# Softmax on 16 rows a head, bands placed by one-hot matmuls, and the first tokens loaded as fp32 by SyncE: a lightweight convolution with a ReGLU layer behind it

## The chip, the cores and the metric

The kernel runs on one core of one Trainium2 chip. The time is in device microseconds, from launch to end of one execution, and smaller is better. The time before is 772.24 us, the median of three runs (771.73 to 774.05).

A core has five engines that run beside each other and wait for one another by semaphores: PE (TensorE, the matmuls), DVE (VectorE), ACT (ScalarE), POOL (GpSimd) and SP (SyncE, which here only issues DMAs). POOL, SP and ACT each have a DMA queue. A DMA that SP or ACT issues copies without a change of type; one that POOL issues can turn fp32 into fp16 on its way.

## The reference

Each head has seven taps. They go through a softmax and are the weights of a causal convolution along the tokens: one output is the weighted sum of its own token and the six before it. The result goes through a layer with a gate.

```python
# x: (8, 4096, 192), weight: (8, 7); 24 channels to a head
w = np.exp(weight - max over taps); w = w / (sum over taps + 1e-9)
out[b, s, h, g] = sum over k of w[h, k] * x_pad[b, s + k, h, g]      # x_pad has 6 rows of zeros in front
# out as (32768, 192); w_gate, w_val: (192, 1536); w_out: (1536, 192)
y = (np.maximum(out @ w_gate, 0) * (out @ w_val)) @ w_out
```

## The kernel before

**Tiling.** The batch is cut into two halves of four sequences, called streams. A unit is 1024 tokens of both streams; there are 16 units (`NUNIT`), done one after the other. In a unit, `xc` holds the convolution's result in fp16 with channels on partitions: 64 channels of the one stream on partitions 0 to 63 and of the other on 64 to 127, three chunks of 64 channels (`NCH`). So each weight tile `Wg` and `Wv` has to be there twice, on partitions 0 to 63 from HBM and copied to 64 to 127 (`both_halves`, L165).

**One unit on PE.** `gate_val` (L465) runs over two windows of 512 tokens and in each over 12 pieces f of 128 hidden columns. For each f, 6 matmuls with `Wg` and 6 with `Wv` fill two PSUM tiles; ACT makes `gr`, the ReLU of the first (L487), DVE multiplies it by the second into `hT` (L488). Then `project_columns` (L491) multiplies `hT` with `Wo` in three parts, and DVE turns each part out (`turn_out`, L512). The last unit is projected in another form (L534). All PSUM tiles come from one pool of four, each of two banks, and are given out in turn: a tile is free again when the engine that reads it is done.

**Convolution, two ways.** The first two units are convolved on PE: a band matrix for each head holds the taps on seven diagonals, and a matmul with a block of 118 or 128 tokens (112 new ones) gives the sums. For the first unit this is `conv_dense` (L256), once for each window: `conv_dense(0)` ahead of everything, `conv_dense(1)` in `gate_val` ahead of f = 7. For the second unit it is `conv(2)` and `conv(3)` (L294), after which ACT moves the sums (L317) and SP issues transposing DMAs into `xc` (L336). All later units are done in lanes, away from PE: POOL loads `x_e` (L350), copies it into `x_p` (L387), SP issues eight transposing DMAs into `x_r` (L389; one more for the tokens ahead of the unit, from `turned`, L382), ACT and DVE multiply `x_r` by `tap` (L435, L415, L446), POOL adds products (L424). `tap` holds the softmax by channel; twenty small DMAs on SP fill it from `late` (L210), a copy of the softmax that POOL makes.

**The start.** POOL loads x for the first window into `out_s` as fp16 (L94, L101). `wr`, the taps repeated over 32 rows a head, comes on two queues (L112). `softmax` (L180) makes `we`; `prod` and `blk` (L223, L231) spread it over diagonals, with `eye` from POOL; sixteen copies of 32 or fewer rows, ten on DVE and six on ACT (L242, L244), put `blk` into `band`. Meanwhile PE runs sixteen matmuls on zeros (L128). The weights come in five steps of columns (`CUTS`), all issued on POOL; DVE copies the halves of the first two steps, POOL of the others.

**What sets the order.** The schedule is manual: each engine does its instructions in the order in which the program lists them, and a waiting instruction holds up everything behind it on its engine, DMA issues too.

Of the kernel before, what the change touches and what calls it, by code (L numbers as in the profile page):

```python
# [8 lines left out]
FP = mybir.dt.float32  # L9
F16 = mybir.dt.float16  # L10
ACTF = mybir.ActivationFunctionType
# [4 lines left out]
def kernel(  # L16
# [27 lines left out]
    TAPS = [(6, 5, 4), (3, 2), (1, 0)]  # L44
    GSUB = 5


# [25 lines left out]
    def staged(i, j):  # L73
        return stages[i][:, XH * j : XH * (j + 1)]

    def load_x(g):


        bp, toks = GROUPS[g]
        xt = staged(g // 3, g % 3).rearrange("p (j s d) -> p j s d", s=2, d=D)  # L80
        if toks[0] == 0:
            nc.vector.memset(xt[0:32, 0, :, :], 0.0)
        for st in range(2):
            b = bp + NB * st
            jj = int(toks[0] == 0)
            last = toks[-1] == S - SUB or toks[-1] - toks[-2] != SUB
            n_full = len(toks) - jj - int(last)
            lo = toks[jj] - PAD
# [5 lines left out]
            nc.gpsimd.dma_start(out=xt[:, jj : jj + n_full, st, :], in_=src)  # L94
# [5 lines left out]
        for st in range(2 * int(toks[0] == 0)):  # L100
            nc.gpsimd.dma_start(  # L101
                out=xt[PAD:128, 0, st, :], in_=x[bp + NB * st, 0 : 128 - PAD, :]
            )
        return xt

    xts = {}
    xts[0] = load_x(0)

    HQ = H // 4
    wr = const.tile([128, HQ, KW], FP)  # L110
    for half, eng in ((0, nc.sync), (1, nc.scalar)):
        eng.dma_start(  # L112
            out=wr[64 * half : 64 * half + 64],
            in_=bass.AP(
                tensor=weight.tensor,
                offset=weight.offset + 2 * half * HQ * KW,
                ap=[[HQ * KW, 2], [0, 32], [1, HQ * KW]],
            ),
        )
    BW = 32 + PAD  # L120
    ones = const.tile([128, BW + PAD], FP)
    nc.vector.memset(ones[:], 1.0)

    zeros = const.tile([128, 512], F16)
    nc.vector.memset(zeros[:], 0.0)
    ps = psum.tile([128, 2, 512], FP, name="ps")
    for n in range(16):
        nc.tensor.matmul(  # L128
            out=ps[:, n % 2, :], lhsT=zeros[:, 0:128], rhs=zeros[:], start=True, stop=True
        )  # L130

    bands = [const.tile([128, 2 * HQ, SUB], F16, name=f"band{half}") for half in range(2)]
    for half in range(2):
        nc.vector.memset(bands[half][:], 0.0)

    eye = const.tile([128, BW + PAD], FP)
    for q in range(4):
        nc.gpsimd.affine_select(  # L140
            out=eye[32 * q : 32 * q + 32],
            in_=ones[32 * q : 32 * q + 32],
            pattern=[[-1, BW + PAD]],
            compare_op=ALU.is_equal,
            fill=0.0,
            base=PAD,
            channel_multiplier=1,
        )
# [16 lines left out]
    def both_halves(copy, s, dst):  # L165
        cols = slice(CUTS[s], CUTS[s + 1])
        copy(out=dst[64:128, :, cols], in_=dst[0:64, :, cols])  # L167
# [12 lines left out]
    def softmax(e, raw, n):  # L180
        mx = const.tile([128, n, 1], FP, name=f"mx{n}")
        nc.vector.tensor_reduce(out=mx[:], in_=raw[:], axis=mybir.AxisListType.X, op=ALU.max)
        nc.vector.tensor_tensor(
            out=e[:], in0=raw[:], in1=mx[:].to_broadcast([128, n, KW]), op=ALU.subtract
        )
        nc.scalar.activation(e[:], e[:], ACTF.Exp)
        sm = const.tile([128, n, 1], FP, name=f"sm{n}")
        nc.vector.tensor_reduce(out=sm[:], in_=e[:], axis=mybir.AxisListType.X, op=ALU.add)
        nc.vector.tensor_scalar(out=sm[:], in0=sm[:], scalar1=1e-9, scalar2=None, op0=ALU.add)  # L189
        nc.vector.reciprocal(sm[:], sm[:])  # L190
        nc.vector.tensor_tensor(
            out=e[:], in0=e[:], in1=sm[:].to_broadcast([128, n, KW]), op=ALU.mult
        )

    we = const.tile([128, HQ, KW], FP)
    softmax(we, wr, HQ)

    tap = const.tile([128, NCH, KW], FP)

    def load_taps():  # L200
        late = const.tile([128, HQ, KW], FP)
        nc.gpsimd.tensor_copy(out=late[:], in_=we[:])
        for c in range(NCH):
            r0 = 0
            while r0 < 64:
                h = (64 * c + r0) // G
                r1 = min(64, G * (h + 1) - 64 * c)
                for half in range(2):
                    p0 = 32 * (h // HQ)
                    nc.sync.dma_start(  # L210
                        out=tap[64 * half + r0 : 64 * half + r1, c, :],
                        in_=late[p0 : p0 + r1 - r0, h % HQ, :],
                    )
                r0 = r1

    load_taps()
    xts[2] = load_x(2)
    pool_halves(4)

    prod = const.tile([128, HQ, BW, KW], FP)  # L220
    e0 = eye[:, 0:1]
    w0 = we[:, 0:1, 0:1]
    nc.vector.tensor_tensor(  # L223
        out=prod[:],
        in0=bass.AP(tensor=e0.tensor, offset=e0.offset, ap=[e0.ap[0], [0, HQ], [1, BW], [1, KW]]),
        in1=bass.AP(tensor=w0.tensor, offset=w0.offset, ap=[w0.ap[0], [KW, HQ], [0, BW], [1, KW]]),
        op=ALU.mult,
    )
    blk = const.tile([128, HQ, BW, 1], F16)
    with nc.allow_low_precision("one of the terms is not zero"):  # L230
        nc.vector.tensor_reduce(out=blk[:], in_=prod[:], axis=mybir.AxisListType.X, op=ALU.add)  # L231

    for q in range(4):
        for j in range(4):
            s0 = 32 * j - PAD
            lo, hi = max(0, -s0), min(BW, SUB - s0)
            rows = min(32, SUB + PAD - 32 * j)
            src = blk[32 * q : 32 * q + rows, :, lo:hi, 0]
            h0 = q % 2 * HQ
            dst = bands[q // 2][32 * j : 32 * j + rows, h0 : h0 + HQ, s0 + lo : s0 + hi]  # L240
            if j < 2 or (j == 2 and q % 2 == 0):
                nc.vector.tensor_copy(out=dst, in_=src)  # L242
            else:
                nc.scalar.copy(out=dst, in_=src)  # L244

    def band(h):
        return bands[h // (2 * HQ)][0 : SUB + PAD, h % (2 * HQ), :]

# [6 lines left out]

    def conv_dense(g):  # L256


        xt = xts.pop(g)
        if g == 0:  # L260
            xc[0] = xcpool.tile([128, NCH, UNIT], F16, name="xc")
        t0 = GROUPS[g][1][0]
        rows = SUB + PAD
        if g == 0:
            both_halves(nc.vector.tensor_copy, 0, Wg)
            both_halves(nc.vector.tensor_copy, 0, Wv)
        for c in range(NCH):
            ps = psum.tile([128, 2, 512], FP, name="ps")
            for jj in range(GSUB):
                col = SUB * jj  # L270
                n = min(SUB, WIN - col)
                for second in range(2):
                    for st in range(2):
                        for k2 in range(2):
# [6 lines left out]
                                lhsT=xt[0:rows, jj, st, 32 * k : 32 * k + m],  # L281
                                rhs=band(h)[:, 0:n],
                                start=True,
# [3 lines left out]
                            )  # L287
            copy = nc.vector.tensor_copy if c == 1 else nc.scalar.copy
            copy(out=xc[0][:, c, t0 : t0 + WIN], in_=ps[:, 0, :])  # L289
        if g == 0:  # L290
            both_halves(nc.vector.tensor_copy, 1, Wg)
            both_halves(nc.vector.tensor_copy, 1, Wv)

# [259 lines left out]

    conv_dense(0)
    lane_load(2)
# [76 lines left out]
```

## Time and profile before

| what | value |
|---|---|
| median of three runs | 772.24 us (771.73 to 774.05) |
| the profiled run | 772.0 us, span 770.3 us |
| PE busy | 762.6 us, 99% of the span |
| DVE, ACT, POOL busy | 674.6, 596.8, 425.6 us |
| granted PE clock | 1.00 |
| gate and value matmuls of one unit | 31.19 us |
| projection of one unit | 15.65 us |
| first matmul that isn't on zeros | 9.22 us after the span's start |
| first gate matmul | 11.20 us |
| gate and value of the first unit end | 46.39 us |

The span is the profiled execution from first to last instruction; the run's own time has some 1.7 us around it. The page also has the busy share of every engine in 40 slices: PE is at nine tenths or more in all but the first and the last, in which it has 7 and 8. A row of a timeline reads: start, length, engine, line, operation, output and input with their shapes, and in brackets how long the engine stood idle before and what released it. In the chain of waits a row is start, length, and what the end of the program was waiting for then. In a row on one line of the code, the three numbers are the shortest, median and longest duration in ns.

### The profile page before, as it was taken

The page shows a single profiled execution, that of the slowest core. Times are in us where ns is not written, and L with a number is a line of the kernel's source. Part 1 is how long each engine was busy: PE and PEld are TensorE (multiplying, and loading weights), DVE is VectorE, ACT ScalarE, POOL GpSimd, SP SyncE. Part 2 cuts the span into 40 slices and gives each one's busy share as a digit, 9 for nine tenths or more (in the row PEclk, how much of TensorE's full clock was granted, in tenths as well). Part 3 has the DMA queues.
Part 4 walks back from the last instruction along what each step waited for, and adds up shares of the span by engine and source line. Part 5 has one row for each costly group of instructions (what it writes and reads, how often), then busy time and mean ns, then how long its engine had stood idle before and what let it go on. Part 6 is the DMA issues. An engine that isn't in the chain of part 4 may idle for free.

```text
span 770.3 us, 21536 instructions
## 1 busy us (share of the span) xinstructions
PE 762.6 (99%) x9392; PEld 381.7 (50%) x9392; DVE 674.6 (88%) x641; ACT 596.8 (77%) x621; POOL 425.6 (55%) x194
## 2 busy tenths in 40 slices
PE   7999999999999999999999999999999999999998
PEld 3654444444444444444444444444444444444448
DVE  7888989989899898999989899898998989996691
ACT  4798787978879787787877879788796877874471
POOL 9606839286490955919368292863919558091000
PEclk9999999999999999999999999999999999999999
DMA  9955819085290933909147090742909232030302
GB/s 113 124 69 102 127 25 143 2 115 51 52 116 2 133 34 77 90 3 146 21 93 73 21 146 2 115 52 44 122 3 126 41 73 52 3 83 3 83 2 83
DMA packets 123106, 53.20 MB, mean 69 GB/s; under 512 B 88692, under 2 KB 123012, under 8 KB 123012
## 3 DMA queue, kind: packets, MB, share of 16 engines
q1 hardware_dynamic: 84690, 36.99, 29.6%
q0 software_dynamic: 38112, 14.75, 18.7%
q8 instruction: 73, 1.20, 0.7%
q14 instruction: 21, 0.17, 0.1%
q10 hardware_dynamic: 210, 0.10, 0.0%
HBM read 29.50 MB, written 25.17 MB: 71 GB/s over the span
## 4 chain that ended last, share of the span: by engine, by line
PE 97%; DVE 1%; DMA 1%; ACT 0%; issue 0%; DVEq 0%
PE ps L478 65%; PE ps L498 30%; PE ps L534 2%; DMA wr<-in_weight_dram 1%; PE ps L304 0%; DVE band L242 0%; DVE Wg L167 0%; DVE Wv L167 0%; DVE hT L488 0%; ACT gr L487 0%; DVE prod L223 0%; DVE blk L231 0%; DVE xc L289 0%; ACT out_s L545 0%; DVE sm L189 0%
## 5 line engine op out<-in xcount | busy, mean ns | idle before, releaser
L487 ACT ACTIVATE gr<-ps 128x1024 f16<-128x1024 f32 x384 | 392.8, 1023 | 148.4 <-PE ps L478 148.4
L488 DVE TENSOR_TENSOR hT<-gr,ps 128x1024 f16<-128x1024 f16 x384 | 468.8, 1221 | 37.5 <-ACT gr L487 8.9
L424 POOL TENSOR_TENSOR prod<-prod,prod 128x1792 f32<-128x1792 f32 x70 | 278.4, 3977 | 258.2 <-DVE prod L456 212.9
L478 PE MATMUL ps<-xc,Wg 64*128 64x512 f16 x2304 | 314.2, 376 | 0.6 <-DVE hT L488 0.2
L478 PE MATMUL ps<-xc,Wv 64*128 64x512 f16 x2304 | 314.1, 376 | 0.6 <-DVE Wv L167 0.3
L498 PE MATMUL ps<-hT,Wo 128*32 128x512 f16 x4320 | 236.0, 379 | 0.0
L478 PEld LDWEIGHTS <-Wv 64*128 64x128 f16 x2304 | 131.8, 94 | 118.5 <-issue 1.3
L478 PEld LDWEIGHTS <-Wg 64*128 64x128 f16 x2304 | 114.4, 94 | 137.1 <-issue 7.0
L498 PEld LDWEIGHTS <-Wo 128*32 128x32 f16 x4320 | 114.1, 97 | 120.3 <-issue 6.3
L415 ACT ACTIVATE prod<-x_r,tap 128x1024 f32<-128x1024 f16 (+1 forms) x182 | 172.8, 1040 | 0.0
L446 DVE SCALAR_TENSOR_TENSOR acc<-x_r,tap,acc 128x1024 f32<-128x1024 f16 (+1 forms) x140 | 114.0, 873 | 2.8 <-ACT acc L435 2.8
L512 DVE STREAM_TRANSPOSE out_s<-ps 128x1024 f32<-128x1024 f32 x45 | 56.2, 1248 | 33.1 <-PE ps L498 33.1
L424 POOL TENSOR_TENSOR xc<-prod,prod 128x1792 f16<-128x1792 f32 x14 | 55.7, 3982 | 1.1
L387 POOL COPY x_p<-x_e 128x1536 f16<-128x1536 f16 x28 | 40.3, 1466 | 2.0 <-DMA x_e<-in_x_dram 2.0
L350 POOL DMA_DIRECT2D x_e<-in_x_dram x28 | 25.0, 899 | 3.8 <-POOL x_p L387 3.6
L446 DVE SCALAR_TENSOR_TENSOR xc<-x_r,tap,acc 128x1024 f16<-128x1024 f16 (+1 forms) x28 | 23.5, 882 | 0.0
L435 ACT ACTIVATE acc<-x_r,tap 128x1024 f32<-128x1024 f16 (+1 forms) x28 | 21.5, 820 | 0.8 <-DMA x_r<-x_p 0.8
L534 PE MATMUL ps<-Wo,hT 128*128 128x192 f16 x192 | 16.0, 246 | 0.0
L534 PEld LDWEIGHTS <-hT 128*128 128x128 f16 x192 | 15.8, 98 | 0.4 <-issue 0.4
L545 ACT COPY out_s<-ps 128x768 f32<-128x768 f32 (+2 forms) x5 | 3.2, 638 | 12.7 <-PE ps L534 12.7
L545 DVE COPY out_s<-ps 128x192 f32<-128x192 f32 x1 | 0.4, 357 | 13.3 <-PE ps L534 13.3
L456 DVE TENSOR_SCALAR prod<-x_r,tap 128x768 f32<-128x768 f16 x14 | 8.7, 618 | 0.0
(45 smaller groups left out, 66.7 us busy)
## 6 DMA issues: line engine op xcount, KB each, us to landing
out_dram<-out_s SPq DMA_DIRECT2D x63, 384.0 KB
x_e<-in_x_dram POOLq DMA_DIRECT2D x28, 384.0 KB, 10.5
x_r<-x_p SPq DMA_TRANSPOSE x112
out_s<-in_x_dram POOLq DMA_DIRECT2D x4, 240.0 KB, 6.2
out_s<-in_x_dram POOLq DMA_DIRECT2D x4, 192.0 KB, 5.0
Wo<-in_moe_w_out_dram POOLq DMA_DIRECT2D x1, 576.0 KB, 8.8
Wg<-in_moe_w_gate_dram POOLq DMA_DIRECT2D x3, 144.0 KB, 4.4
Wv<-in_moe_w_val_dram POOLq DMA_DIRECT2D x3, 144.0 KB, 4.8
```

The source lines that it names most:

```text
L350: nc.gpsimd.dma_start(out=xe[:, :, st, :, :].rearrange("p j c r -> p j (c r)"), in_=bass.AP(tensor=x.tensor, offset=x.offset + row * D, ap ...
L387: nc.gpsimd.tensor_copy(out=xp[:, :, :, st, :], in_=xe[:, :, st, :, :])
L415: nc.scalar.activation(out=prods[u, k][:, at - LDVE : at - LDVE + n], in_=shifted(u, c, k, t, n), func=ACTF.Copy, scale=tap[:, c, k : k + 1],)
L424: nc.gpsimd.tensor_tensor(out=p0[:] if k < KW - 1 else flat(u)[:, LDVE:FLAT], in0=p0[:], in1=prods.pop((u, k))[:], op=ALU.add,)
L435: nc.scalar.activation(out=accs[u][:, at : at + n], in_=shifted(u, c, 0, t, n), func=ACTF.Copy, scale=tap[:, c, 0:1],)
L446: nc.vector.scalar_tensor_tensor(out=(flat(u) if k == KW - 1 else acc)[:, at : at + n], in0=shifted(u, c, k, t, n), scalar=tap[:, c, k : k ...
L478: nc.tensor.matmul(out=pss[i][:, st, :], lhsT=W[64 * st : 64 * st + 64, c, 128 * f : 128 * (f + 1)], rhs=xcb[64 * st : 64 * st + 64, c, WI ...
L487: nc.scalar.activation(out=gr[:], in_=pss[0][:], func=ACTF.Relu)
L488: nc.vector.tensor_tensor(out=h[:, f], in0=gr[:], in1=pss[1][:], op=ALU.mult)
L498: nc.tensor.matmul(out=ps[32 * s : 32 * s + 32, b, :], lhsT=Wo[:, f, 64 * p + 32 * b : 64 * p + 32 * b + 32], rhs=hs[s // 2][:, f, s % 2, ...
L512: nc.vector.transpose(out=o[:, :, 64 * p : 64 * p + 64].rearrange("p t (b c) -> p b t c", b=2), in_=ps[:].rearrange("p b (t c) -> p b t c" ...
L534: nc.tensor.matmul(out=ps[:, i // 2, D * (i % 2) : D * (i % 2) + D], lhsT=h[:, f, st, 128 * q : 128 * (q + 1)], rhs=Wo[:, f, :], start=(f ...
```

## The change

It works on the start and on what the first unit does beside it.

- The taps `w` are repeated over 16 rows a head (128 rows for 8 heads) by one DMA on ACT's queue. Maximum, `Exp` and sums run on 7 columns; the sum's reciprocal is folded into `blocks`.
- A one-hot matrix `Z` shifts `blocks` on PE: after two matmuls of zeros that open the banks, eight matmuls for each half of the heads add up the bands in two PSUM tiles; DVE copies one half to `bands`, ACT the other. The sixteen small copies are gone.
- The first window's x is loaded as fp32 by SP in five DMAs and cast on ACT (three) and DVE (two). POOL's queue begins with the weights, in other cuts.
- Six matmuls on zeros (`WARM`) instead of sixteen.
- DVE copies the halves of the first weight step only, POOL those of the next four; those of the last 256 columns are copied by two DMAs on SP, ahead of the taps. They wait for the last weight load.
- `tap` is filled from `wn` (ACT) by 32 DMAs of 16 or 8 rows.
- `conv_dense(1)` runs one chunk each ahead of f = 9, 10 and 11; its x is loaded later, one stream at a time; `load_x(2)` stands behind it.

```diff
+    WARM = 6
+    STEPS0 = [1, 0, 2, 3, 4]
+    CONV1 = [9, 10, 11]
...
-    xts[0] = load_x(0)
...
-    for half, eng in ((0, nc.sync), (1, nc.scalar)):
-        eng.dma_start(
-            out=wr[64 * half : 64 * half + 64],
...
+    def load_raw(jj):
+        lo = SUB * jj - PAD
+        p0 = max(0, -lo)
+        nc.sync.dma_start(
+            out=raw[jj][p0 : ROWS[jj], :].rearrange("p (s d) -> p s d", s=2),
...
+    def cast(copy, jj):
+        copy(
+            out=xts[0][0 : ROWS[jj], jj, :, :].rearrange("p s d -> p (s d)"),
+            in_=raw[jj][0 : ROWS[jj], :],
+        )
...
+    nc.scalar.dma_start(
+        out=w[:],
+        in_=bass.AP(tensor=weight.tensor, offset=weight.offset, ap=[[KW, H], [0, HR], [1, KW]]),
+    )
+    for jj in STEPS0:
+        load_raw(jj)
...
-    for n in range(16):
+    for _ in range(WARM):
         nc.tensor.matmul(
-            out=ps[:, n % 2, :], lhsT=zeros[:, 0:128], rhs=zeros[:], start=True, stop=True
+            out=held[:, 0, :], lhsT=zeros[:, 0:128], rhs=zeros[:], start=True, stop=True
...
-    CUTS = [0, 128, 384, 768, 1152, DFF]
+    CUTS = [0, 128, 256, 512, 896, DFF]
+    HALVES = [0, 128, 256, 512, 896, 1280, DFF]
...
-    for s in range(4):
+    for s in range(5):
         load_w(s)
-    xts[1] = load_x(1)
+    pool_halves(1)
+    xts[1] = load_x(1, [0])
     pool_halves(2)
-    load_w(4)
     pool_halves(3)
...
+    load_x(1, [1])
+    pool_halves(4)
...
+    nc.scalar.activation(out=e[:, 0:KW], in_=w[:], func=ACTF.Exp, bias=mx[:])
+    cast(nc.scalar.copy, 1)
+    cast(nc.scalar.copy, 0)
...
+    nc.vector.scalar_tensor_tensor(
+        out=blocks[:],
+        in0=blk[:].to_broadcast([128, H, BW]),
+        scalar=sm[:],
+        in1=mask[:].to_broadcast([128, H, BW]),
+        op0=ALU.mult,
+        op1=ALU.mult,
+    )
+    wn = const.tile([128, KW], FP)
+    nc.scalar.activation(out=wn[:], in_=e[:, 0:KW], func=ACTF.Copy, scale=sm[:])
+    cast(nc.scalar.copy, 2)
...
+    for half, copy in enumerate((nc.vector.tensor_copy, nc.scalar.copy)):
+        for j in range(128 // HR):
+            s0 = HR * j - PAD
+            lo, hi = max(0, -s0), min(BW, SUB - s0)
+            nc.tensor.matmul(
...
+                lhsT=Z[:, 112 - HR * j : 240 - HR * j],
+                rhs=blocks[:, H // 2 * half : H // 2 * (half + 1), lo:hi],
+                start=False,
...
+        copy(
+            out=bands[half][:].rearrange("p h t -> p (h t)"), in_=raised[half][:, 0, 0 : SUB * H // 2]
+        )
+    cast(nc.vector.tensor_copy, 3)
+    cast(nc.vector.tensor_copy, 4)
...
     def load_taps():
-        late = const.tile([128, HQ, KW], FP)
-        nc.gpsimd.tensor_copy(out=late[:], in_=we[:])
+        both_halves(nc.sync.dma_start, 5, Wg)
+        both_halves(nc.sync.dma_start, 5, Wv)
...
-                for half in range(2):
-                    p0 = 32 * (h // HQ)
-                    nc.sync.dma_start(
-                        out=tap[64 * half + r0 : 64 * half + r1, c, :],
-                        in_=late[p0 : p0 + r1 - r0, h % HQ, :],
-                    )
+                for st in range(2):
+                    for a in range(r0, r1, HR):
+                        n = min(HR, r1 - a)
+                        nc.sync.dma_start(
+                            out=tap[64 * st + a : 64 * st + a + n, c, :],
+                            in_=wn[HR * h : HR * h + n, :],
+                        )
                 r0 = r1
...
-            if u == 0 and w == 0 and f == 7:
-                conv_dense(1)
+            if u == 0 and w == 0 and f in CONV1:
+                conv_dense(1, [CONV1.index(f)])
...
-    conv_dense(0)
+    xc[0] = xcpool.tile([128, NCH, UNIT], F16, name="xc")
+    both_halves(nc.vector.tensor_copy, 0, Wg)
+    both_halves(nc.vector.tensor_copy, 0, Wv)
+    conv_dense(0, range(NCH))
+    xts[2] = load_x(2)
```

More of the change, by code (lines that the diff above doesn't have):

```diff
@@ L74, in staged, with load_x @@
         return stages[i][:, XH * j : XH * (j + 1)]
-    def load_x(g):
+    def load_x(g, streams=range(2)):
         bp, toks = GROUPS[g]
         xt = staged(g // 3, g % 3).rearrange("p (j s d) -> p j s d", s=2, d=D)
-        if toks[0] == 0:
-            nc.vector.memset(xt[0:32, 0, :, :], 0.0)
-        for st in range(2):
+        for st in streams:
             b = bp + NB * st
-            jj = int(toks[0] == 0)
             last = toks[-1] == S - SUB or toks[-1] - toks[-2] != SUB
-            n_full = len(toks) - jj - int(last)
-            lo = toks[jj] - PAD
+            n_full = len(toks) - int(last)
+            lo = toks[0] - PAD
             src = bass.AP(
@@ L93, in load_x @@
             )
-            nc.gpsimd.dma_start(out=xt[:, jj : jj + n_full, st, :], in_=src)
+            nc.gpsimd.dma_start(out=xt[:, 0:n_full, st, :], in_=src)
             if last:
@@ L99, in load_x @@
                 )
-        for st in range(2 * int(toks[0] == 0)):
-            nc.gpsimd.dma_start(
-                out=xt[PAD:128, 0, st, :], in_=x[bp + NB * st, 0 : 128 - PAD, :]
-            )
-        return xt
-    xts = {}
-    xts[0] = load_x(0)
-    HQ = H // 4
-    wr = const.tile([128, HQ, KW], FP)
-    for half, eng in ((0, nc.sync), (1, nc.scalar)):
-        eng.dma_start(
-            out=wr[64 * half : 64 * half + 64],
+        return xt
+    xts = {0: staged(0, 0).rearrange("p (j s d) -> p j s d", s=2, d=D)}
@@ L114 @@
+    ROWS = [SUB + PAD, 128, 128, 128, 80]
+    raw = [
+        apool.tile([128, FLAT - LDVE], FP, name=f"prod{jj + 1}")[:, 0 : 2 * D] for jj in range(GSUB)
+    ]
+    def load_raw(jj):
[3 more added lines that the diff above has]
+            out=raw[jj][p0 : ROWS[jj], :].rearrange("p (s d) -> p s d", s=2),
             in_=bass.AP(
-                tensor=weight.tensor,
-                offset=weight.offset + 2 * half * HQ * KW,
-                ap=[[HQ * KW, 2], [0, 32], [1, HQ * KW]],
-            ),
-        )
@@ L120 @@
-    BW = 32 + PAD
-    ones = const.tile([128, BW + PAD], FP)
-    nc.vector.memset(ones[:], 1.0)
+                tensor=x.tensor,
+                offset=x.offset + (lo + p0) * D,
+                ap=[[D, ROWS[jj] - p0], [NB * S * D, 2], [1, D]],
+            ),
+        )
+    def cast(copy, jj):
[3 more added lines that the diff above has]
+        )
+    HR = 128 // H
+    BW = HR + PAD
+    w = const.tile([128, KW], FP)
@@ L124 @@
+    nc.scalar.dma_start(
[4 more added lines that the diff above has]
+        load_raw(jj)
     zeros = const.tile([128, 512], F16)
     nc.vector.memset(zeros[:], 0.0)
-    ps = psum.tile([128, 2, 512], FP, name="ps")
-    for n in range(16):
+    e = const.tile([128, KW + 1], FP)
+    nc.vector.memset(e[:, KW:], 1e-9)
+    Z = const.tile([128, 256], F16)
+    nc.vector.memset(Z[:], 0.0)
+    nc.vector.memset(raw[0][0:PAD, :], 0.0)
@@ new lines @@
+    early = const.tile([128, 1], FP)
+    nc.scalar.activation(out=early[:], in_=e[:, KW:], func=ACTF.Exp)
+    ones = const.tile([128, 128], FP)
+    nc.gpsimd.memset(ones[:], 1.0)
+    eye = const.tile([128, 128], FP)
+    nc.gpsimd.affine_select(
+        out=eye[:],
+        in_=ones[:],
+        pattern=[[-1, 128]],
+        compare_op=ALU.is_equal,
+        fill=0.0,
+        base=0,
+        channel_multiplier=1,
+    )
+    mask = const.tile([128, H, 1], FP)
+    with nc.allow_low_precision("one of the terms is not zero"):
+        nc.vector.tensor_reduce(
+            out=Z[:, 112 : 112 + HR],
+            in_=eye[:].rearrange("p (g i) -> p i g", i=HR),
+            axis=mybir.AxisListType.X,
+            op=ALU.add,
+        )
@@ L128 @@
+    nc.vector.tensor_reduce(
+        out=mask[:, :, 0],
+        in_=eye[:].rearrange("p (g i) -> p g i", i=HR),
+        axis=mybir.AxisListType.X,
+        op=ALU.add,
+    )
+    held = psum.tile([128, 2, 512], FP, name="ps")
+    for _ in range(WARM):
         nc.tensor.matmul(
-            out=ps[:, n % 2, :], lhsT=zeros[:, 0:128], rhs=zeros[:], start=True, stop=True
+            out=held[:, 0, :], lhsT=zeros[:, 0:128], rhs=zeros[:], start=True, stop=True
         )
-    bands = [const.tile([128, 2 * HQ, SUB], F16, name=f"band{half}") for half in range(2)]
+    raised = [psum.tile([128, 2, 512], FP, name="ps") for _ in range(2)]
@@ L133 @@
     for half in range(2):
[L134 to L147, printed above, removed]
+        nc.tensor.matmul(
+            out=raised[half][:, 0, 0 : SUB * H // 2],
+            lhsT=zeros[:, 0:128],
+            rhs=zeros[:, 0 : SUB * H // 2],
+            start=True,
+            stop=False,
+            skip_group_check=True,
@@ L165, in both_halves @@
     def both_halves(copy, s, dst):
-        cols = slice(CUTS[s], CUTS[s + 1])
+        cols = slice(HALVES[s], HALVES[s + 1])
         copy(out=dst[64:128, :, cols], in_=dst[0:64, :, cols])
@@ L171, in pool_halves @@
         both_halves(nc.gpsimd.tensor_copy, s, Wv)
-    for s in range(4):
+    for s in range(5):
         load_w(s)
-    xts[1] = load_x(1)
+    pool_halves(1)
+    xts[1] = load_x(1, [0])
     pool_halves(2)
-    load_w(4)
     pool_halves(3)
[L180 to L184, printed above, removed]
-        )
[L186 to L193, printed above, removed]
@@ L195 @@
-    we = const.tile([128, HQ, KW], FP)
-    softmax(we, wr, HQ)
+    load_x(1, [1])
+    pool_halves(4)
+    mx = const.tile([128, 1], FP)
+    nc.vector.tensor_reduce(
+        out=mx[:], in_=w[:], axis=mybir.AxisListType.X, op=ALU.max, negate=True
+    )
+    nc.scalar.activation(out=e[:, 0:KW], in_=w[:], func=ACTF.Exp, bias=mx[:])
+    cast(nc.scalar.copy, 1)
+    cast(nc.scalar.copy, 0)
+    prod = const.tile([128, BW, KW], FP)
+    z0 = Z[:, 112 - PAD : 113 - PAD]
+    e0 = e[:, 0:1]
+    nc.vector.tensor_tensor(
+        out=prod[:],
+        in0=bass.AP(tensor=z0.tensor, offset=z0.offset, ap=[z0.ap[0], [1, BW], [1, KW]]),
+        in1=bass.AP(tensor=e0.tensor, offset=e0.offset, ap=[e0.ap[0], [0, BW], [1, KW]]),
+        op=ALU.mult,
+    )
@@ new lines @@
+    blk = const.tile([128, 1, BW], FP)
+    nc.vector.tensor_reduce(out=blk[:, 0, :], in_=prod[:], axis=mybir.AxisListType.X, op=ALU.add)
+    sm = const.tile([128, 1], FP)
+    nc.vector.tensor_reduce(out=sm[:], in_=e[:], axis=mybir.AxisListType.X, op=ALU.add)
+    nc.vector.reciprocal(sm[:], sm[:])
+    blocks = const.tile([128, H, BW], F16)
+    nc.vector.scalar_tensor_tensor(
[5 more added lines that the diff above has]
+        op1=ALU.mult,
+    )
@@ new lines @@
+    wn = const.tile([128, KW], FP)
+    nc.scalar.activation(out=wn[:], in_=e[:, 0:KW], func=ACTF.Copy, scale=sm[:])
+    cast(nc.scalar.copy, 2)
+    bands = [const.tile([128, H // 2, SUB], F16, name=f"band{half}") for half in range(2)]
+    for half, copy in enumerate((nc.vector.tensor_copy, nc.scalar.copy)):
+        for j in range(128 // HR):
+            s0 = HR * j - PAD
+            lo, hi = max(0, -s0), min(BW, SUB - s0)
+            nc.tensor.matmul(
+                out=raised[half][:, 0, 0 : SUB * H // 2].rearrange("p (h t) -> p h t", t=SUB)[
+                    :, :, s0 + lo : s0 + hi
+                ],
+                lhsT=Z[:, 112 - HR * j : 240 - HR * j],
+                rhs=blocks[:, H // 2 * half : H // 2 * (half + 1), lo:hi],
+                start=False,
+                stop=(j == 128 // HR - 1),
+                skip_group_check=True,
+            )
+        copy(
+            out=bands[half][:].rearrange("p h t -> p (h t)"), in_=raised[half][:, 0, 0 : SUB * H // 2]
+        )
@@ L207, in load_taps @@
                 r1 = min(64, G * (h + 1) - 64 * c)
-                for half in range(2):
-                    p0 = 32 * (h // HQ)
-                    nc.sync.dma_start(
-                        out=tap[64 * half + r0 : 64 * half + r1, c, :],
-                        in_=late[p0 : p0 + r1 - r0, h % HQ, :],
-                    )
+                for st in range(2):
[4 more added lines that the diff above has]
+                            in_=wn[HR * h : HR * h + n, :],
+                        )
                 r0 = r1
     load_taps()
[L217 to L244, printed above, removed]
     def band(h):
-        return bands[h // (2 * HQ)][0 : SUB + PAD, h % (2 * HQ), :]
+        return bands[h // 4][0 : SUB + PAD, h % 4, :]
     xc = {}
@@ L254, with conv_dense @@
     PLACE |= {6: (1, 0, 0), 7: (1, 0, 1), 2: (1, 1, 0), 5: (1, 1, 1)}
[L256 to L261, printed above, removed]
+    def conv_dense(g, chunks):
+        xt = xts[g]
         t0 = GROUPS[g][1][0]
         rows = SUB + PAD
[L264 to L267, printed above, removed]
+        for c in chunks:
             ps = psum.tile([128, 2, 512], FP, name="ps")
-            for jj in range(GSUB):
+            for jj in STEPS0:
                 col = SUB * jj
                 n = min(SUB, WIN - col)
+                rows = n + PAD
                 for second in range(2):
@@ L281, in conv_dense @@
                                 lhsT=xt[0:rows, jj, st, 32 * k : 32 * k + m],
-                                rhs=band(h)[:, 0:n],
+                                rhs=band(h)[0:rows, 0:n],
                                 start=True,
@@ L287, in conv_dense @@
                             )
-            copy = nc.vector.tensor_copy if c == 1 else nc.scalar.copy
+            copy = nc.vector.tensor_copy if c == 1 and g == 0 else nc.scalar.copy
             copy(out=xc[0][:, c, t0 : t0 + WIN], in_=ps[:, 0, :])
-        if g == 0:
-            both_halves(nc.vector.tensor_copy, 1, Wg)
-            both_halves(nc.vector.tensor_copy, 1, Wv)
     def conv(g):
```

## The prediction, made before the changed kernel ran

> **What bounds the kernel now.** I read the page's head first (PE busy 762.6 of a span of 770.3 us: what a change can win lies in the few microseconds in which PE waits), then the chain of waits in order of time, which says where those are.
>
> ```profile
> 0.81 4.33 DMA wr<-in_weight_dram
> ...
> 6.92 0.73 DVE prod L223
> ...
> 7.67 0.72 DVE blk L231
> ...
> 11.21 0.69 DVE xc L289
> ...
> 11.93 1.12 DVE Wg L167
> ...
> 13.26 1.24 DVE Wv L167
> ...
> 14.54 6.66 PE ps L478 x59
> ...
> 64.11 31.19 PE ps L478 x288
> ```
>
> The reader sees that 14.5 us of DMA and VectorE come first, and that from then on the chain is PE, in equal pieces (31.19 gate and value, 15.65 projection). So an earlier start of PE ought to shift the end by as much, if nothing behind it is late. I therefore looked for the next engine that has no room: ScalarE between the first unit's last `gr` and the second unit's first (its timeline), and SyncE, whose queue feeds it (its timeline).
>
> ```profile
> 46.98 2.00 ACT L317 CAST out_s<-ps 112x480 f16<-112x480 f32 x5 [0.17 <-PE ps L304]
> 49.00 1.55 ACT L435 ACTIVATE acc<-x_r,tap 128x1024 f32<-128x1024 f16 x2
> 50.46 5.69 ACT L415 ACTIVATE prod<-x_r,tap 128x768 f32<-128x768 f16 x6
> 56.05 1.96 ACT L317 CAST out_s<-ps 112x480 f16<-112x480 f32 x5
> 57.89 6.75 ACT L415 ACTIVATE prod<-x_r,tap 128x768 f32<-128x768 f16 x7
> 64.91 1.02 ACT L487 ACTIVATE gr<-ps 128x1024 f16<-128x1024 f32 x1 [0.26 <-PE ps L478]
> ```
> ```profile
> 17.94 14.74 SPq L210 DMA_DIRECT2D tap<-late  x20
> 32.81 1.20 SPq L382 DMA_TRANSPOSE x_r<-turned  x1
> 34.12 10.87 SPq L389 DMA_TRANSPOSE x_r<-x_p  x8
> ```
>
> ScalarE works without a gap from 46.98 to 64.64 and is free 0.27 us before PE needs it. Its `acc` at 49.00 needs all `x_r` transposes; the last is issued by 45.0 (34.12 + 10.87) and the DMA view of 34 to 50 us shows its bytes until about 45.8, so `x_r` is there 2 to 3 us early. Before the transposes on the same queue stand the twenty tap loads. This is the path on which the change can lose what it wins.
>
> **The start, part by part.** (1) `w` comes as one load on ScalarE's queue beside x on SyncE's. `wr` lands for 5.14 now; ScalarE's issue alone lasts until 1.95 and the DMA view of 2 to 6 us shows first bytes at 2.2, so between 3.2 and 5.1: I take 4.2, in the middle, as both queues share the engines. Gain 1.0 (0 to 2).
> (2) From `mx` to the third-last step. Before, `mx` starts at 5.24 and the second chunk's first gate matmul at 11.95: 6.7 us. After: six small VectorE steps and one `Exp`; `prod` and its reduction shrink from 532 to 154 elements (0.71 us; 0.17 for 14 elements; so 0.32 each), `mx`, `sm`, reciprocal 0.17 each, `Exp` 0.21, `blocks` of 176 elements 0.35; with seven hand-overs of 0.03 that is 1.9. Eight one-hot matmuls, which no row shows: between 0.083 each (128x192 at L534: 16.0/192) and 0.43 (a warm-up), I take 0.11, for they are narrow, 0.9. Band copy of 448 columns 0.6 (0.69 for 512 at L289, DVE). Then VectorE does two casts of x (0.45 each, as `Wg` 64x384: 0.49 and `Wv`: 0.42), the two halves (0.9) and `xc` (0.69): 1.9 + 0.9 + 0.6 + 0.9 + 0.9 + 0.7 + 0.2 = 6.1. Gain 0.6. ScalarE's casts (0.45 each) fit beside this while x is there.
> (3) The VectorE copies of 64x768 (L167: 1.40 and 1.23) go to GpSimd as 64x384 (a third of its 1.14 each). From 11.95, four pairs of 0.217 and one f of 1.30 would have ended at 14.12; the next f began at 14.98. Gain 0.9. GpSimd, after ten weight issues of 0.63 each from about 2.0, copies at 8.5 to 9.5; the second f comes at about 11. Its later copies end some 0.5 to 1 us before they are needed; without that cover a stall of that size.
> (4) The dense pieces move from f = 7 to f = 9, 10, 11: the same 1.6 us of matmuls; small waits either way (0.2 and 0.28 stand in the rows around 23.5 and 25.3). Zero.
> (5) SyncE's five x issues (rows 0.32 to 2.14 for stores, 0.75 for `wr`) are over by 6 and delay nothing on SyncE, which then waits for weights.
> PE would so be about 2.5 us earlier (0.5 to 3.9).
>
> One more thing on PE: the eight warm-ups last 6 x 0.43 + 2 x 0.37 = 3.3 us, and PE then idles until the one-hot matmuls, at about 6. In this trace the weight loads of the warm-ups come every 0.43 us until 6.61, then three in 0.54 us: the matmuls double their rate 5.1 us after the first one (the profile's granted clock is 1.00 throughout). The Trainium skill's page "TensorE: Matmul & The Clock Gate", Part 1 (The HAM clock gate) says that the full clock comes after about 3.4 us of sustained activity, in a window that runs free of the kernel; by that rule the shorter warm-up may leave the dense pieces and first gates at half rate. The trace agrees with the delay; nothing here shows what a pause does. Priced from rows: dense at half rate costs 1.6 more, the first f 1.3 more, so 3 at most, and PE would be 0.5 late instead of 2.5 early. I keep it as a rival.
>
> **What is behind it: SyncE.** The taps were released by GpSimd at 17.72 (`late`). Now they stand behind two SBUF copies of the last weight columns, which wait for the last weight load, and there are 32 of them instead of 20. When does that load land? Weights are 2 x 576 KB (page, part 6), 1.18 MB, and moved at 150 GB/s between 8.2 and 13.5 us, so 7.9 us; x as fp32 is 576 rows x 2 x 768 bytes = 0.88 MB at the 325 GB/s of a plain store (757 to 758 us), 2.7 us. The rate was full only from 5.0 now; from 2.2 at the earliest. So the last weights land at 12.8 to 15.6; I take 14.5. The Trainium skill's page "DMA: Bandwidth & Descriptors", section "Issuing engines are not separate DMA queues", says that loads from several queues share the same 16 engines; by it x on SyncE's queue brings the weights no earlier than the sum of bytes does, which is the sum that I made. The trace agrees as far as it goes: DMA share at 9 tenths or more from 5 to 13 us with GpSimd's queue alone.
> Second copy 0.6: taps from 15.1. Their price:
>
> ```profile
> L210 SPq DMA_DIRECT2D tap<-late x2: 583/588/593, 21.1 to 21.7; - x2
> L210 SPq DMA_DIRECT2D tap<-late x3: 643/643/714, 26.0 to 27.5; - x3
> ```
>
> The first row is two loads of 16 rows, the second (its 643) two of 8 rows. With 0.045 between, 16 x 0.63 + 16 x 0.69 = 21.1. Each waits for the load eight before it, issued 5.3 earlier; issue to landing of `x_e` is 5.4 to 6.5 in that stretch, and a tap load is small beside it: I add 0.3 (0 to 1.2 for each of three rounds). So 15.1 + 21.4 = 36.5 (before 32.7), `turned` 1.3, eight transposes 10.9, bytes and semaphore 1.5 (1 to 2): `x_r` is there at 50.2. GpSimd's `x_p`, 32.9 now, is earlier and not the bound.
>
> `acc` on ScalarE then starts at 50.2, not 49.0; behind it stand 6 products, the moves of conv(3), 7 products and the second unit's first `gr`, which PE waits for two f later through the PSUM tiles. Room there: 0.25. **Sum:** the end moves by 50.2 - 49.0 - 0.25 = +0.95, whatever PE won before, for it waits at about 64. Span 771.3; the profiled run was 1.7 above its span (772.0) and the median of the three runs 0.24 above that: 773.2.
>
> **The rivals.** What counts as no change is 0.3%, 2.3 us: 769.9 to 774.6.
> A, the taps come early: the DMA engines are full from 2.2 and the weights, of which the last have wider rows, move at the 177 GB/s seen from 5.0 to 7.2 us: 2.2 + 2.7 + 6.7 = 11.6; then 0.6 + 20.6 + 1.3 + 10.6 + 1.0 makes 45.7, before ScalarE wants `x_r` (46.5). The gain of the start comes through, 2.5: 769.7. For it: a queue that doesn't wait for GpSimd may fill the engines sooner. Against it: it needs every term at its low end, and weights moved at 150.
> B, slower: the tap loads wait for one another. Issue to landing rose to 6.5 for `x_e` and 8.8 for `Wo`, which will be in flight with them; at 6.3 a round of eight instead of 5.3, three rounds cost 1 each (2.7 over the 0.3 taken), and the weights at 15.1 add 0.6: `x_r` at 53.5, the end at +4.2: 776.4. It decides (over 774.6) from `x_r` at 51.6. Against it: before, the twenty loads took 14.74 where their issues with the gaps sum to 14.6.
> C, PE at half rate: it shows only where PE loses more than 2.5 + 0.95 = 3.4 us, above the 3 priced; with a second and third f at half rate (1.3 each) 5.6 are lost and the end is at +3.1: 775.3. For it: the idle 1 to 2 us after the warm-ups. Against it: PE is busy again from about 6.
> D, the start is no earlier (`w` at 5.1, no more): hidden behind the same wait, the forecast's time.
>
> **How the numbers follow.** Forecast (with D) 0.50, A 0.19, B 0.27, C 0.04. So faster 0.19, no change 0.50, slower 0.31. Predicted 773.2; its own range 771 to 774.6 (the landing of weights and of `x_r`, each about 1 us); it reaches to A and to B, 769.7 to 776.4.
>
> **What would show it.** Right: the last weight load lands near 14.5, taps run from 15 to 36 on SyncE, ScalarE's first `acc` waits for the DMA of `x_r` for 3 us or more, PE enters conv(2) near 44 and then waits at the second unit's gates for VectorE or ScalarE. Wrong: `acc` follows the conv(2) moves with no wait (then A), a PE that enters conv(2) at 46 or later (C or D), or taps with gaps between them (B).

## The result and the profile after

| | before | after |
|---|---|---|
| median | 772.26 us (771.67 to 774.21, 20 runs) | 774.35 us (771.93 to 776.35, 20 runs) |
| the profiled run, its span | 772.0, 770.3 us | 772.72, 771.0 us |
| first matmul that isn't on zeros | 9.22 us | 6.74 us |
| first gate matmul | 11.20 us | 10.88 us |
| PE enters `conv(2)` | 46.32 us | 44.70 us |
| last tap load issued by | 32.7 us | 36.4 us |
| ScalarE's first `acc` | 49.00 us | 50.29 us |
| last move on ScalarE | 767.04 us | 767.91 us |

The ratio is 1.0024 with a 95% interval of 1.0015 to 1.0033: the changed kernel is slower by a quarter of a per cent, inside the 0.3% that was called no change. PE reaches the end of the first unit 1.6 us earlier, and the end comes 0.7 us later in the profiled run and 2.1 us later by the medians. So something between 45 and 70 us takes back more than was won.

SyncE's timeline of the kernel after (start, length, queue, line, operation, output and input, count):

```profile
12.21 0.72 SPq L205 DMA_DIRECT2D Wg<-Wg  x1
13.42 0.60 SPq L205 DMA_DIRECT2D Wv<-Wv  x1
14.14 22.29 SPq L288 DMA_DIRECT2D tap<-wn  x32
36.53 1.51 SPq L425 DMA_TRANSPOSE x_r<-turned  x1
38.15 11.01 SPq L432 DMA_TRANSPOSE x_r<-x_p  x8
```

The taps start 3.8 us earlier than before (17.94), but there are 32 of them and they take 22.29 us instead of 14.74. The transposes behind them, which ScalarE needs, start at 38.15 and not at 34.12. ScalarE's timeline shows what that does:

```profile
45.35 2.00 ACT L360 CAST out_s<-ps 112x480 f16<-112x480 f32 x5 [0.17 <-PE ps L347]
50.29 1.55 ACT L478 ACTIVATE acc<-x_r,tap 128x1024 f32<-128x1024 f16 x2 [2.94 <-DMA x_r<-x_p]
51.74 5.70 ACT L458 ACTIVATE prod<-x_r,tap 128x768 f32<-128x768 f16 x6
57.34 1.96 ACT L360 CAST out_s<-ps 112x480 f16<-112x480 f32 x5
59.18 6.75 ACT L458 ACTIVATE prod<-x_r,tap 128x768 f32<-128x768 f16 x7
65.84 2.94 ACT L530 ACTIVATE gr<-ps 128x1024 f16<-128x1024 f32 x3
```

The bracket of `acc` is the new wait: ScalarE has its `conv(2)` moves done at 47.35 and stands idle for 2.94 us until the last transpose has landed. From there to 68.8 it works without a gap, so the 2.94 us are not made up, and the second unit's first `gr` starts at 65.84 instead of 64.91. PE, which came early, waits there (its timeline, same kernel):

```profile
44.70 1.07 PE L347 MATMUL ps<-out_s,band 118*112 118x240 f16 x8
...
65.12 0.82 PE L521 MATMUL ps<-xc,Wv 64*128 64x512 f16 x6 [0.57 <-DVE out_s L555]
66.89 0.82 PE L521 MATMUL ps<-xc,Wg 64*128 64x512 f16 x6 [0.95 <-ACT gr L530]
68.15 0.82 PE L521 MATMUL ps<-xc,Wv 64*128 64x512 f16 x6 [0.43 <-DVE hT L531]
```

In the kernel before, PE came to the same places at these times:

```profile
46.32 1.07 PE L304 MATMUL ps<-out_s,band 118*112 118x240 f16 x8
...
67.30 0.81 PE L478 MATMUL ps<-xc,Wv 64*128 64x512 f16 x6
```

The first unit's gain is spent in these three waits. Groups that don't wait start 0.65 us after one another; these three start 1.39, 1.77 and 1.26 us after the group ahead of them. That is 2.47 us more, the 1.62 that PE had won and 0.85 beyond. The chain of waits tells the same: before, it ran over PE from 14.54 us on; now it goes over SyncE's queue, ScalarE and VectorE, and joins PE at 68.15.

```profile
19.40 5.98 DMA tap<-wn
25.40 6.01 DMA tap<-wn
...
47.20 3.06 DMA x_r<-x_p
50.29 1.55 ACT acc L478 x2
...
68.15 28.02 PE ps L521 x258
```

The two `tap` rows are new too. In the trace the program's DMAs on SyncE take eight semaphores in turn, and a tap load isn't issued until the load eight before it, which has the same semaphore, has landed. That took 6.0 us from its issue, and eight issues in a row take only some 5.2, so the queue stands still for the rest.

### The profile page after: what moved, and what is told of

Same layout as the page of the kernel before. It is cut to its first block, busy times and chain, and to the rows that moved or that the text cites. A ratio compares the mean times of both kernels' runs of the same rounds, so it can differ in the third digit from the quotient of the medians.

```text
span 771.0 us, 21553 instructions
## 1 busy us (share of the span) xinstructions
PE 761.9 (99%) x9400; PEld 379.8 (49%) x9400; DVE 669.8 (87%) x630; ACT 598.1 (78%) x622; POOL 422.5 (55%) x189
## 4 chain that ended last, share of the span: by engine, by line
PE 91%; SPq 3%; DMA 3%; ACT 2%; issue 0%; DVE 0%
PE ps L521 60%; PE ps L541 28%; PE ps L577 2%; DMA tap<-wn 2%; ACT prod L458 2%; SPq L288 1%; SPq L432 1%; DMA prod<-in_x_dram 1%; DMA x_r<-x_p 0%; ACT gr L530 0%; PE ps L325 0%; SPq L111 0%; ACT out_s L360 0%; ACT acc L478 0%; SPq L425 0%
## 5 line engine op out<-in xcount | busy, mean ns | idle before, releaser
L521 PEld LDWEIGHTS <-Wg 64*128 64x128 f16 x2304 | 112.2, 94 | 138.6 <-issue 7.9
L588 DVE COPY out_s<-ps 128x192 f32<-128x192 f32 x1 | 0.4, 358 | 13.3 <-PE ps L577 13.3
```

What stands on the lines that cost most here:

```text
L521: nc.tensor.matmul(out=pss[i][:, st, :], lhsT=W[64 * st : 64 * st + 64, c, 128 * f : 128 * (f + 1)], rhs=xcb[64 * st : 64 * st + 64, c, WI ...
```

## The experiments

Two theories were set against each other. The queue theory: the end follows the arrival of `x_r` through SyncE's tap loads, whatever the start does. The rival, the clock theory: the start costs it, since the granted PE clock is at half for part of the dense convolution in the changed kernel. The windows of the kernel after show that this is so (PE, PEld, DVE, ACT and POOL busy, then the granted clock, the share of the DMA engines, in which the times of all packets are added up, so that it can pass 1, and GB/s):

```profile
4.55:7.97 3.42, 0.97 (x25) 0.78 (x27) 2.05 (x7) 2.40 (x6) 2.70 (x6) 1.00 1.31 245
...
8.00:9.00 1.00, 0.92 (x40) 0.55 (x38) 0.81 (x3) 0.03 (x1) 0.74 (x2) 0.50 1.39 195
9.00:10.00 1.00, 1.00 (x56) 1.00 (x60) 0.93 (x2) 0.59 (x1) 1.00 (x3) 0.50 1.32 203
10.00:11.00 1.00, 1.00 (x50) 0.89 (x40) 0.69 (x1) 0.01 (x1) 1.00 (x2) 0.50 1.22 210
11.00:12.00 1.00, 1.00 (x10) 0.37 (x9) 0.00 (x0) 0.58 (x1) 1.00 (x2) 0.81 1.18 205
```

The first row is a stretch in which PE was busy for 0.97 of 3.42 us; the clock stands at 0.50 right after it. The experiments ran in two groups, each beside the kernel before on its own chip (772.17 us in both groups; 772.26 in the group of the kernel after).

### Some taps ahead of the copies

```diff
-        both_halves(nc.sync.dma_start, 5, Wg)
-        both_halves(nc.sync.dma_start, 5, Wv)
+        issued = 0
...
+                        if issued == 12:
+                            both_halves(nc.sync.dma_start, 5, Wg)
+                            both_halves(nc.sync.dma_start, 5, Wv)
+                        issued += 1
```

> The changed kernel with the two SBUF copies of the last weight columns put behind the twelfth tap load, so that SyncE issues taps from about 6.7 us and not from 14.1. Queue theory (the end follows the arrival of x_r): x_r is there at 44 to 46 us, ScalarE's first acc follows the conv(2) moves at about 47.3 with no wait for a DMA, and the start of PE comes through: 1.6 us under the kernel before, 770.6 us, ratio 0.998. Clock theory (what is lost is PE at half rate in the start) or any other that leaves the queue out: as the changed kernel, 774.4, ratio 1.0024.

Measured: 770.88 us (769.63 to 772.01, 11 runs), ratio 0.9979 (0.9969 to 0.9989). Its timelines of SyncE and of ScalarE:

```profile
6.39 8.48 SPq L291 DMA_DIRECT2D tap<-wn  x12
14.99 0.72 SPq L205 DMA_DIRECT2D Wg<-Wg  x1
...
16.50 13.99 SPq L291 DMA_DIRECT2D tap<-wn  x20
...
33.40 11.10 SPq L435 DMA_TRANSPOSE x_r<-x_p  x8
```
```profile
47.12 2.00 ACT L363 CAST out_s<-ps 112x480 f16<-112x480 f32 x5 [0.17 <-PE ps L350]
48.98 1.59 ACT L481 ACTIVATE acc<-x_r,tap 128x1024 f32<-128x1024 f16 x2
```

The same DMAs in another order: the first twelve taps run while the last weights are still on their way, the transposes start 4.8 us earlier, and `acc` follows the moves with no wait. That alone turns the slower kernel into one that is 0.2% faster than before. The next bound is near: the transposes now start as GpSimd's `x_p` is done, at 33.38, and stand 1.2 us for it behind `turned`. The profiled execution is the longest of the eleven (772.01). It has two stretches at half clock, from 8.24 to 15.07 us, and PE enters `conv(2)` only at 46.47: here, where the queue is out of the way, the clock does cost. The three executions with the lowest mean clock (0.995) are the three longest, 771.55 to 772.01.

### Eight more loads behind the taps

```diff
     load_taps()
+    spare = const.tile([128, NCH, KW], FP)
+    for n in range(8):
+        nc.sync.dma_start(out=spare[16 * n : 16 * n + 16, 0, :], in_=wn[16 * n : 16 * n + 16, :])
```

> The changed kernel with eight more loads of 16 rows behind the taps on SyncE, into a tile that nobody reads. Queue theory: x_r is 5 to 6 us later, ScalarE waits 8 to 9 us for it instead of 2.9, and the end is 5 to 6 us later: about 779.8, ratio 1.0098. Clock theory: no change against the changed kernel, 774.4.

Measured: 780.59 us (779.76 to 781.51, 4 runs), ratio 1.0108 (1.0095 to 1.0121). ScalarE's timeline:

```profile
46.47 2.00 ACT L363 CAST out_s<-ps 112x480 f16<-112x480 f32 x5 [0.17 <-PE ps L350]
59.09 1.55 ACT L481 ACTIVATE acc<-x_r,tap 128x1024 f32<-128x1024 f16 x2 [10.62 <-DMA x_r<-x_p]
```

The eight loads took 6.05 us on the queue and the median rose by 6.24 over that of the kernel after: by the medians, what is put on SyncE ahead of the transposes comes out at the end of the program, one for one. The wait of `acc` was expected at 8 to 9 us and is 10.62, with `acc` 8.80 later than in the kernel after. This is the longest execution of its four against the second shortest of twenty there: its taps started 1.0 later (15.15), and `acc` started 2.87 us after the end of the last transpose's issue instead of 1.13.

### Eleven warm-up matmuls

```diff
-    WARM = 6
+    WARM = 11
```

> The changed kernel with eleven warm-up matmuls instead of six, so that PE is busy until about 6.7 us. Both theories: the granted clock stays at 1.00 through the dense pieces, which then take about 1.2 us less, and PE enters conv(2) at about 43.4 instead of 44.7. Queue theory: ScalarE waits for x_r that much longer and the end stays, 774.4 (within 0.7). Clock theory: the end is 1.2 to 1.7 us earlier, 772.9.

Measured: 774.14 us (772.24 to 776.05, 12 runs), ratio 1.0021 (1.0012 to 1.0031), the same as the changed kernel. The granted clock is 1.00 through the dense convolution now. Rows of PE's timeline (the last dense matmuls and `conv(2)`), ScalarE's `acc` and SyncE's taps:

```profile
9.75 1.15 PE L325 MATMUL ps<-band,out_s 70*32 70x64 f16 x88 [0.49 <-DVE out_s L121]
...
44.69 1.07 PE L347 MATMUL ps<-out_s,band 118*112 118x240 f16 x8
```
```profile
52.88 1.55 ACT L478 ACTIVATE acc<-x_r,tap 128x1024 f32<-128x1024 f16 x2 [5.53 <-DMA x_r<-x_p]
```
```profile
14.88 24.01 SPq L288 DMA_DIRECT2D tap<-wn  x32
```

So the clock theory falls for the changed kernel: with the half clock gone, the time stays. PE isn't earlier at `conv(2)` (44.69 to 44.70, where 43.4 was expected), because the dense matmuls now wait for x instead. So this run does not test what an earlier PE would be worth alone; that the start isn't the cause rests on the queue experiments. The profiled execution is the longest of its twelve (776.05), and the rows say why: the taps started 0.74 later than in the kernel after and took 24.01 us instead of 22.29. In its chain of waits one of them took 8.35 us to land, against 6.0:

```profile
20.68 8.35 DMA tap<-wn
```

The queue stood still for 2.12 us on that one, against 1.86 in three waits in the kernel after. Most of the 1.7 us lies in the issues themselves, 20.56 us in sum against 19.19; the longest is that same load's, 1.49.

### Both edits

The first edit and `WARM = 11` together.

> Taps first and eleven warm-ups together. Queue theory: with x_r early, the clock counts: 1.2 us under the kernel with the taps first alone, about 769.4, ratio 0.9963. Clock theory: as eleven warm-ups alone, 772.9.

Measured: 770.04 us (769.34 to 770.34, 5 runs), ratio 0.9970 (0.9958 to 0.9982): the fastest of all, 0.3% below the kernel before. Its timelines of ScalarE and PE:

```profile
45.19 2.00 ACT L363 CAST out_s<-ps 112x480 f16<-112x480 f32 x5 [0.17 <-PE ps L350]
47.05 1.59 ACT L481 ACTIVATE acc<-x_r,tap 128x1024 f32<-128x1024 f16 x2
```
```profile
44.54 1.07 PE L350 MATMUL ps<-out_s,band 118*112 118x240 f16 x8
```

Nothing waits between `conv(2)` and the second unit's gates, and the last move on ScalarE is at 765.26, 1.78 before that of the kernel before: just what PE won at `conv(2)` (46.32 - 44.54). The warm-ups seem to be worth something here that they weren't worth alone: 0.84 us between the medians, and no run beyond 770.34. With five runs this is not clear of the noise, as the two intervals overlap.

### The kernel before with more taps

The kernel before as it stood, and 3 or 12 loads of 8 rows more behind its twenty taps.

```diff
     load_taps()
+    spare = const.tile([128, NCH, KW], FP)
+    for n in range(3):
+        nc.sync.dma_start(out=spare[8 * n : 8 * n + 8, 0, :], in_=we[8 * n : 8 * n + 8, 0, :])
```

> The kernel before, with three more 8-row loads behind its twenty taps on SyncE, into a tile that nobody reads (its result stays the reference's). Queue theory: three loads cost 3 x 0.69 = 2.1 us on SyncE, x_r lands at 48 instead of 46 and ScalarE's acc wants it at 49.0, so nothing changes: 772.2 us (771.8 to 772.9), acc starts at 49.0 with no wait or one under 0.3 us. Rival (the kernel before has no room on this queue either, its end follows the taps directly): +2.1 less the 0.27 us at the gate, 774.0 us.

> The kernel before, with twelve more 8-row loads behind its twenty taps on SyncE, into a tile that nobody reads; now as many loads as the changed kernel has, at an unchanged start of the program. Queue theory: 12 x 0.69 = 8.3 us more on the queue, x_r lands at 54 to 55.3, acc waits 5 to 6.3 us for its DMA, the end moves by that less 0.27: 777 to 778.5 us, and PE stalls at the second unit's gates near 65 to 72. Rival (the loss of the changed kernel comes from its start, clock or late x, and the taps are hidden): 772.2 us.

Measured: with three 772.05 us (771.88 to 774.98, 11 runs), ratio 1.0007 (0.9998 to 1.0017); with twelve 777.35 us (776.68 to 778.98, 5 runs), ratio 1.0069 (1.0055 to 1.0083). ScalarE's `acc` in the one and in the other:

```profile
49.66 1.55 ACT L438 ACTIVATE acc<-x_r,tap 128x1024 f32<-128x1024 f16 x2 [0.72 <-issue]
```
```profile
55.02 1.55 ACT L438 ACTIVATE acc<-x_r,tap 128x1024 f32<-128x1024 f16 x2 [6.04 <-DMA x_r<-x_p]
```

With three loads `acc` starts 0.66 later than before, in a wait that the trace does not name, and the time does not move: the kernel before has room on this queue, and three loads use it up. The wait was expected at under 0.3 us; the eight transposes took 11.94 us instead of 10.87, which wasn't foreseen. Their issue ends at 48.49, 1.17 ahead of `acc`, as in the kernel after (1.13), so the wait is probably the landing of `x_r`. With twelve loads the start of the program is the old one, and still the time rises by 5.2 us. So the number of small loads is enough to make the kernel slower, with no part of the change at the start.

### All five together

The prediction's rule was that the end moves by what `acc` starts after 49.0 + 0.25. Against the profiled runs' own times (772.0 before):

| kernel | `acc` starts | by the rule | measured |
|---|---|---|---|
| before, three loads more | 49.66 | +0.4 | +0.05 |
| after | 50.29 | +1.0 | +0.7 |
| after, eleven warm-ups | 52.88 | +3.6 | +4.05 |
| before, twelve loads more | 55.02 | +5.8 | +5.35 |
| after, eight loads more | 59.09 | +9.8 | +9.5 |

The rule holds within 0.5 us over a range of nine, in kernels with the old start and with the new. It speaks only of an `acc` that is late. With the taps first `acc` starts at 48.98 and with both edits at 47.05, ahead of 49.25, and there the end follows PE: 772.01 and 770.07 in the profiled runs, with PE in `conv(2)` at 46.47 and 44.54.

## Why the prediction was right, and where its sizes were off

The forecast was no change, 773.2 us, with the taps on SyncE as the cause; measured are 774.35 us, and the cause is shown by the experiments. Step by step:

- **The place of the end.** `acc` waiting 3 us or more for `x_r`, PE in `conv(2)` near 44 and then waiting at the second unit's gates for VectorE or ScalarE: the trace has 2.94 us (a little under what was asked), 44.70, and the three waits from 65 to 68 us.
- **`x_r` at 50.2.** Measured 50.29 for the start of `acc`, but by errors that cancel. The last weights were put at 14.5, and SyncE's second copy went at 13.42, so the taps started at 14.14 instead of 15.1. The taps were put at 21.4 and took 22.29: the issues were some 0.7 cheaper than 21.1, and the waits for the load eight before, put at 0.3, were 1.9 (gaps of 0.81, 0.53 and 0.52 us in the row of issues). That the total came out at 50.2 is luck. (The DMA share, read as nine tenths or more from 5 to 13 us, has three slices of five or six tenths in that view.)
- **The median.** The profiled run, 772.72, was forecast at 773.0 and is the second lowest of its twenty; the median is 1.6 above it, only 0.25 under the top of the forecast's range, and eight of the twenty lie above that top. The term that was mis-sized in the profiled run is "I add 0.3 (0 to 1.2 for each of three rounds)", 1.9 instead, and gaps between the taps are the sign that the prediction gave for rival B. Rival B's 776.4 is the time of the longest runs (776.35). What makes the others longer than the profiled one is not shown, since they were not profiled. The nearest trace is the long one with eleven warm-ups, which has the same queue: its `acc` is 2.6 later than in the kernel after, by later weights (0.74), dearer issues of the taps (1.4) and only some 0.3 more of waiting. The clock is not needed for the spread: with eleven warm-ups every execution has a mean clock of 0.998 or more, and they lie as far apart (772.24 to 776.05).
- **PE 2.5 earlier.** It was 1.6. Gain by `w`: 0.46 instead of 1.0 (`mx` at 4.78, not at 4.2). From `mx` to the second chunk's first gate: 6.76 instead of 6.1 (before 6.71), no gain. The prediction took x to be there ("while x is there"), and it wasn't: see the rows below. The copies that left VectorE: the third f starts at 13.71 instead of 14.98, 0.86 more than the 0.41 won by then, as put (0.9). The dense pieces, put at zero, and the small waits up to `conv(2)`: 0.35 won. None of it shows in the time, as was said.
- **One-hot matmuls.** 0.11 us each was taken, 0.9 for eight; the sixteen took 0.73, and VectorE started the first band's copy at 7.21, when half of them were done.
- **Rival A** (the taps come early, 769.7) did not occur in this kernel; the first experiment makes it occur by order alone, 770.88. **Rival C** (half clock) occurred, at 8 to 11.4 us, and cost nothing in the time, since its price of at most 3 us lies under the wait for `x_r`, as the prediction's condition had it.

The Trainium skill's page "TensorE: Matmul & The Clock Gate", Part 1 (The HAM clock gate), has the clock go back to half after an idle window of about 3.4 us; the prediction had left open what a pause does. The trace agrees in the length: 0.50 from 7.97 to 11.38 us, 3.41 us. It differs in the condition: the window ahead of it (4.55 to 7.97) was not idle, PE was busy for 0.97 of it.

PE's and VectorE's timelines of the kernel after, for the start:

```profile
6.74 0.73 PE L259 MATMUL ps<-blocks,Z 128*128 128x64 f16 x16 [2.02 <-DVE blocks L242]
7.89 3.05 PE L325 MATMUL ps<-band,out_s 118*32 118x112 f16 x120 [0.43 <-DVE band L269]
...
11.54 0.38 PE L521 MATMUL ps<-xc,Wg 64*128 64x512 f16 x2
```
```profile
4.78 0.16 DVE L221 TENSOR_REDUCE mx<-w 128x1 f32<-128x7 f32 x1 [2.69 <-DMA w<-in_weight_dram]
...
8.06 0.82 DVE L121 CAST out_s<-prod 128x384 f16<-128x384 f32 x2 [0.22 <-DMA prod<-in_x_dram]
```

The same matmuls in PE's timeline of the kernel before:

```profile
9.22 2.04 PE L279 MATMUL ps<-band,out_s 118*32 118x112 f16 x120 [1.58 <-ACT band L244]
```

The first band is ready 1.3 us earlier than before (7.89 against 9.22), but the dense matmuls take 3.05 us instead of 2.04: the last two steps of x are cast only when their DMA is in, and the clock is at half. With the clock at full (both edits) VectorE's last cast of x is later still, at 9.16 after 0.57 us of waiting for its DMA, and the second chunk's gate comes at 11.38, 6.80 after `mx`. So the late x is enough to hold the old length.

## What to carry to other kernels

Where PE is busy from end to end, as here, a faster start is worth only what the slowest queue behind it leaves: look for the first instruction on another engine that needs a DMA queue's last transfer, and count how much of that queue's work is small loads ahead of it. In these programs a small DMA cost its issue (0.51 us or more) and, from the ninth on, sometimes a wait for the landing of the one eight before, whose semaphore it shares. Where small loads don't depend on a late transfer, put them ahead of the copies that do: here order alone made up for what the change had added to the queue.

## What the runs showed of the hardware that was not expected

- The granted clock changed in steps of 3.41 us, and each step went with how long PE had been busy in the step before. Cut the eight profiles into stretches of 3.413 us that fit their changes of the clock. From full, it fell after stretches with PE busy for 0.65 us (eight loads more, at 61.2, when PE had stood still since 58.4), 0.97 (the kernel after, at 7.97) and 1.21 (taps first, at 8.24), and at the ends of programs after at most 1.29. It stayed at full after 1.51 (the kernel before with twelve loads more, 5.67 to 9.08 us), after 1.71 (the kernel before, 6.62 to 10.03) and after all that were busier. From half it came back after stretches of 3.27 us or more of busy time, but not after 2.44 (taps first, 8.24 to 11.66) or 2.90 (eight loads more, 6.58 to 9.99). So the kernel after lost one stretch, and the same start with the taps first lost two. PE's busy times are modelled, and no experiment was made on this.
- The column of the granted clock says 1.00 also ahead of a profile's first clock record, where the rows show half rate: with eight loads more the pairs of first gates start every 0.43 us until 13.3, and every 0.22 at full clock in the kernel after.
- As GpSimd's first weight loads begin to move, the traffic dips: in the kernel after from 207 GB/s between 2 and 3 us to 55 between 3 and 4, and back to 274 between 5 and 6. The five loads of x are in flight then, and `w` too. In the kernel before, with no x on SyncE, GpSimd's first loads are slow too: 17 to 74 GB/s between 2.9 and 4.8 us, and 165 or more from 5.0. What causes the dip, and what it costs, was not tried.
